# One PSUM tile of eight banks in place of four tiles of two banks, in a block-causal attention followed by a gated convolution layer

## The chip, the cores and the metric

The kernel runs on one core of one Trainium2 chip. The metric is device time in microseconds (us), lower is better: 213.19 us is the median of three runs of the kernel before (213.16 to 213.46).

## What is computed

```python
# attention: q, k, v are (8, 8, 576, 64) fp32
scores = scale * np.matmul(q, k.transpose(0, 1, 3, 2))      # scale = 1/8
mask = block_i >= block_j                                   # blocks of 64 positions
scores = np.where(mask, scores, -1000000000.0)
attn = np.exp(scores - np.max(scores, axis=-1, keepdims=True))
attn = attn / (np.sum(attn, axis=-1, keepdims=True) + 1e-09)
x = np.matmul(attn, v)                  # then reshaped to (8, 576, 512)
# gated layer: a causal convolution of 5 taps per channel makes the gate
gate_pre[:, s] = sum(conv_w[k] * xp[:, s + k] for k in range(5))   # xp: x with 4 rows of zeros ahead
gate = 1.0 / (1.0 + np.exp(-gate_pre))
out = (gate * (x @ w_val)) @ w_out      # w_val, w_out: (512, 512)
```

## The kernel before

The 64 heads are taken as 32 pairs, p = 0 to 31, four pairs to a batch. For two pairs at a time, 576 KB of q and of k are loaded (L171 to L182), cast to fp16 by GpSimd (`cq`, L212), and transposed by VectorE (`tq`, L246); the values come in 128 KB pieces (`Lv`, L191) and are cast by GpSimd (`cv`, L224). TensorE forms scores (`s`, L276) with 32-row tiles of the array, two heads to a pair of PSUM banks. ScalarE takes the exponential of both banks in one instruction (`e`, L288) and writes fp16 to `pt`; GpSimd clears the masked corner of it (`m`, L293 to L298). TensorE multiplies with the values (`av`, L304): 15 matmuls of 65 columns for one head, into one bank, where column 64 is the softmax sum. VectorE normalizes that bank (`n`, L317 a reciprocal `rc`, L318 a multiply into `x`). A pair's result is transposed, by TensorE and a VectorE copy (`xtr`, L325; `xt`, L338) or by a DMA (`xd`, L332), into `xt`.

The gated layer works on ten blocks of rows (`ORDER`, L343). For each, TensorE forms the convolution with diagonal matrices (`cn`, L354, four banks), ScalarE takes a tanh of two banks at a time (`th`, L382), TensorE multiplies with `w_val` (`val`, L386, one bank), VectorE multiplies gate and value (`gv`, L394, out of that bank), TensorE multiplies with `w_out` (`o`, L398, one bank), and ScalarE or VectorE copies the result out (`oc`, L406, which does it in the helper at L230) for the store (`st`, L413). Nearly all matmuls are recorded in the helper `mm`, so they carry L109.

The order of the work is written out by hand, in two strings at the head of the file, `START` and `PLAN`. Each word is one step: `av.13.1@4` is head 1 of pair 13 into bank 4, `val.2.0@5` the first quarter of `val` of block 2 into bank 5, `oc.0.2@A` a copy by ScalarE. The steps are recorded in that order on each engine (`tc.manual_schedule()`), and each engine runs its own in order; an instruction that waits holds up what is behind it on its engine. Which bank is used is thus fixed in the plan. The waits between engines are not written: the framework sets them, from what each instruction reads and writes of each tile.

PSUM has eight banks of 512 fp32 values per partition, 0 to 7. The kernel holds them as four tiles, B0 to B3, of two banks each; all accesses go through three small functions, `f32(i)` and `f16(i)` for one bank and `two(i, j, w)` for a pair of neighbours, which the exponentials and the tanh use:

```python
    def f32(i):
        return BK[i // 2][0:128, i % 2]
...
    def two(i, j, w):
        assert i % 2 == 0 and j == i + 1
        return BK[i // 2][0:128, 0:2, 0:w]
```

Of the kernel before, what the change touches and what calls it, by code (L numbers as in the profile page):

```python
# [87 lines left out]
def kernel(  # L88
# [11 lines left out]
    fp32 = mybir.dt.float32  # L100
# [4 lines left out]
    B, H, SEQ, D = q.shape  # L105
# [10 lines left out]
    psum = ctx.enter_context(tc.tile_pool(name="psum", bufs=1, space=bass.MemoryType.PSUM))  # L116
# [35 lines left out]
    tiny = const([128, 1], fp32, "tiny")  # L152


    BK = [psum.tile([128, 2, 512], fp32, tag=f"B{i}", name=f"B{i}") for i in range(4)]
    bank = {}

    def f32(i):
        return BK[i // 2][0:128, i % 2]

    def f16(i):
        return f32(i).bitcast(fp16)

    def two(i, j, w):
        assert i % 2 == 0 and j == i + 1
        return BK[i // 2][0:128, 0:2, 0:w]


    def load_qk(a, i, m):
# [93 lines left out]
    def steps(a, t, rows, m):  # L263
        qt, kt, z = qT[a % NQT], kT[a % NQT], kz[a % NQT].rearrange("p c g s -> p c (g s)")
        for r, b in zip(rows, m):
            bank["s", a, t, r] = b
        work = (((64, kt, 0, 64, 512), (0, z, 0, 0, 64), (0, z, 64, 512, 576)),
                ((0, kt, 128, 128, 576), (448, kt, 0, 512, 576)),
                ((0, kt, 256, 256, 576), (320, kt, 384, 384, 576)))[t]
        for w, (o, keys, g, x, y) in enumerate(work):  # L270
            for c in range(2):
                yield [(f32(b)[:, o:o + y - x], keys[32 * r:32 * r + 32, c, g:g + 128],
                        qt[32 * r:32 * r + 32, c, x:y], c == 0 and (t, w) != (0, 2), c == 1 and (t, w) != (0, 1))
                       for r, b in zip(rows, m)]
# [12 lines left out]
    def exps(a, t, r, m):  # L287
        nc.scalar.activation(out=pts[(2 * a + r) % NPT][0:128, 0:2, 512 * t:512 * t + 512],  # L288
                             in_=two(bank["s", a, t, 2 * r], bank["s", a, t, 2 * r + 1], 512),
                             func=AF.Exp, bias=0.0, scale=0.125)  # L290
# [13 lines left out]
    def av(p, h, m):  # L304
        b, g = divmod(p, 4)
        bank["av", p, h] = m[0]
        for i in range(5):
            for j in range(i + 1):
                o = last[j] if i == 4 else off[j] + 128 * i
                w = v16t[b % 2][0:128, 2 * g + h, 0:65] if j == 4 else v16s[p % NV][0:128, j, h, 0:65]  # L310
                mm(f32(m[0])[:, 65 * i:65 * i + 65], pts[p % NPT][0:128, h, o:o + 128], w,
                   start=(j == 0), stop=(j == i))
# [67 lines left out]
    def gate(n, r, m):  # L380
        w = width(n)
        nc.scalar.activation(out=ths[ORDER.index(n) % NTH][0:128, 2 * r:2 * r + 2, 0:w],  # L382
                             in_=two(bank["cn", n, 2 * r], bank["cn", n, 2 * r + 1], w),
                             func=AF.Tanh, bias=0.0, scale=0.5)
# [128 lines left out]
```

## Time and profile before

| what | value |
|---|---|
| median of three runs | 213.19 us |
| the profiled execution | 211.73 us |
| its span, first to last instruction | 209.9 us |
| VectorE (DVE) busy | 128.1 us, 61% |
| ScalarE (ACT) busy | 126.7 us, 60% |
| GpSimd (POOL) busy | 100.0 us, 48% |
| DMA queue q1: share of 16 engines' span, MB | 75.4%, 42.26 |
| mean granted clock of TensorE | 0.974 |

PE is TensorE's matmuls, PEld its weight loads, which overlap them; SP issues nearly all DMAs. Times in a timeline are microseconds from the start of the span. A group's "idle before, releaser" is how long the engine had stood still ahead of it, and what ended the longest of those waits. A busy matmul engine includes the drain of the pipeline after each run of matmuls.

### The profile page before, as it was taken

To read this page: it belongs to the slowest core of one execution; us is meant where nothing else is said; L and a number is where in the kernel's file an instruction comes from. 1 tells how busy PE (TensorE), PEld (TensorE's weight loads), DVE (VectorE), ACT (ScalarE), POOL (GpSimd) and SP (SyncE) were. 2 spreads that over 40 slices of the span, in tenths; PEclk is the share of its full clock that TensorE was granted. 3 is DMA by queue.
4 is the path that set the end of the run, shared out by engine and by line. 5 is a ranking of instruction groups with operands and counts; after the bars stand their busy time and mean duration, and the time that the engine had idled before them with its cause. 6 is when DMAs were issued, how large, how long until landed. Compare 5 with 4: busy or idle time off the path is not lost.

```text
span 209.9 us, 7311 instructions
## 1 busy us (share of the span) xinstructions
PE 166.1 (79%) x3082; PEld 101.0 (48%) x3082; DVE 128.1 (61%) x268; ACT 126.7 (60%) x147; POOL 100.0 (48%) x189
## 2 busy tenths in 40 slices
PE   3398679968789768988968878987787898979871
PEld 0235556635545444545555455543543575646430
DVE  2767475877756865766656757547447866562630
ACT  4398846957288736576866366764768685323331
POOL 5379776690391575383845253472345652200000
PEclk9999976999999979999999999999999999999999
DMA  5799899996029799990599579959997548952236
GB/s 143 181 372 277 230 326 359 369 247 226 2 66 245 142 219 323 313 282 10 116 228 323 98 122 297 328 144 107 312 320 204 108 86 228 206 150 101 105 131 169
DMA packets 61067, 43.12 MB, mean 205 GB/s; under 512 B 50917, under 2 KB 51173, under 8 KB 61034
## 3 DMA queue, kind: packets, MB, share of 16 engines
q1 hardware_dynamic: 60762, 42.26, 75.4%
q8 instruction: 24, 0.39, 0.7%
q10 hardware_dynamic: 272, 0.39, 0.6%
q14 instruction: 9, 0.07, 0.1%
HBM read 30.42 MB, written 9.44 MB: 190 GB/s over the span
## 4 chain that ended last, share of the span: by engine, by line
PE 50%; DVE 24%; DMA 11%; issue 4%; ACT 4%; SPq 2%; POOL 2%; DVEq 0%; POOLq 0%; ACTq 0%
PE B L109 49%; DVE x L318 7%; DVE gv L394 6%; DMA qks<-in_q_dram 6%; DVE kT L246 3%; DVE rc L317 3%; DMA vtst<-in_v_dram 2%; ACT osb L230 2%; DVE osb L230 2%; PE B L325 2%; SPq L179 1%; ACT th L382 1%; DMA qks<-in_k_dram 1%; DVE qT L246 1%; DMA vst<-in_v_dram 1%
## 5 line engine op out<-in xcount | busy, mean ns | idle before, releaser
L288 ACT ACTIVATE pt<-B 128x1024 f16<-128x1024 f32 x96 | 92.6, 1025 | 36.2 <-PE B L109 30.4
L230 POOL CAST qk<-qks 128x1152 f16<-128x1152 f32 (+1 forms) x33 | 44.3, 1350 | 23.9 <-DMA qks<-in_k_dram 10.0
L109 PE MATMUL B<-v,pt 128*128 128x65 f16 x896 | 37.7, 197 | 14.4 <-DVE x L318 6.2
L109 PEld LDWEIGHTS <-pt 128*128 128x128 f16 x960 | 36.0, 100 | 21.8 <-issue 14.8
L109 PE MATMUL B<-w_out,gv 128*128 128x512 f16 (+1 forms) x148 | 37.0, 380 | 6.5 <-DVE x L318 3.2
L109 PE MATMUL B<-xt,w_val 128*128 128x512 f16 (+1 forms) x160 | 36.0, 357 | 6.6 <-DVE gv L394 4.5
L109 PE MATMUL B<-qT,kT 32*128 32x448 f16 (+3 forms) x640 | 35.9, 304 | 6.2 <-DVE qT L246 4.1
L394 DVE SCALAR_TENSOR_TENSOR gv<-th,B 128x512 f16<-128x512 f32 (+1 forms) x40 | 24.8, 629 | 18.0 <-PE B L109 14.5
L318 DVE TENSOR_TENSOR x<-B,rc 128x320 f16<-128x320 f32 x64 | 31.5, 492 | 2.2
L317 DVE RECIPROCAL rc<-B 128x5 f32<-128x5 f32 x64 | 12.1, 190 | 29.2 <-PE B L109 26.5
L109 PEld LDWEIGHTS <-kT 32*128 32x128 f16 x640 | 17.2, 96 | 24.1 <-issue 10.4
L296 POOL MEMSET pt<- 64x384 f16 x32 | 13.2, 413 | 29.3 <-ACT pt L288 28.0
L382 ACT ACTIVATE th<-B 128x1024 f32<-128x1024 f32 (+1 forms) x20 | 17.7, 938 | 14.2 <-PE B L109 14.2
L230 ACT COPY osb<-B 128x512 f32<-128x512 f32 (+1 forms) x22 | 12.2, 569 | 22.4 <-PE B L109 18.4
L109 PEld LDWEIGHTS <-w_val 128*128 128x128 f16 x160 | 14.5, 97 | 20.1 <-issue 8.8
L109 PEld LDWEIGHTS <-gv 128*128 128x128 f16 x148 | 13.5, 98 | 19.0 <-issue 8.4
L246 DVE STREAM_TRANSPOSE kT<-qk 128x576 f32<-128x576 f32 (+2 forms) x18 | 20.4, 1131 | 3.4 <-POOL qk L230 3.3
L246 DVE STREAM_TRANSPOSE qT<-qk 128x576 f32<-128x576 f32 (+2 forms) x18 | 20.3, 1130 | 2.4 <-POOL qk L230 1.4
L224 POOL CAST v<-vst 128x512 f16<-128x512 f32 x32 | 19.5, 617 | 4.3 <-DMA vst<-in_v_dram 3.4
L230 DVE COPY osb<-B 128x512 f32<-128x512 f32 x15 | 10.2, 688 | 12.4 <-PE B L325 5.6
L295 POOL COPY pt<-pt 128x128 f16<-128x128 f16 x32 | 9.4, 295 | 11.7 <-ACT pt L288 11.4
L109 PE MATMUL B<-xt,DG 32*32 32x512 f16 (+1 forms) x800 | 13.8, 357 | 0.5 <-DVE x L318 0.3
(44 smaller groups left out, 99.8 us busy)
## 6 DMA issues: line engine op xcount, KB each, us to landing
qks<-in_q_dram SPq DMA_DIRECT2D x15, 576.0 KB, 6.3
qks<-in_k_dram SPq DMA_DIRECT2D x15, 576.0 KB, 5.2
vst<-in_v_dram SPq DMA_DIRECT2D x64, 128.0 KB, 4.6
out_dram<-osb SPq DMA_DIRECT2D x32, 256.0 KB, 3.4
vtst<-in_v_dram SPq DMA_DIRECT2D x8, 128.0 KB, 5.8
w_st<-in_moe_w_val_dram SPq DMA_DIRECT2D x2, 512.0 KB, 5.7
osb<-in_moe_w_out_dram SPq DMA_DIRECT2D x2, 512.0 KB, 7.7
out_dram<-osb SPq DMA_DIRECT2D x6, 128.0 KB, 3.1
```

The costliest lines, as they stand in the source:

```text
L109: nc.tensor.matmul(out=out, lhsT=lhsT, rhs=rhs, start=start, stop=stop, skip_group_check=True)
L224: nc.gpsimd.tensor_copy(out=v16s[p % NV][0:128, 0:4, 0:2, 0:64], in_=vst[p % NVS][0:128])
L230: (eng.copy if eng is nc.scalar else eng.tensor_copy)(out=o, in_=i)
L246: nc.vector.transpose(out=(qT, kT)[i][a % NQT][ps, :, t:t + 32 * w].bitcast(fp32).rearrange("p c (x n) -> p c n x", n=w // 2), in_=qk16[(2 ...
L288: nc.scalar.activation(out=pts[(2 * a + r) % NPT][0:128, 0:2, 512 * t:512 * t + 512], in_=two(bank["s", a, t, 2 * r], bank["s", a, t, 2 * ...
L295: nc.gpsimd.tensor_copy(out=pt[0:128, 0:2, 1536:1600], in_=pt[0:128, 0:2, 0:64])
L296: nc.gpsimd.memset(pt[64:128, 0:2, 0:1536].rearrange("p h (t s) -> p h t s", t=3)[:, :, :, 0:64], 0.0)
L317: nc.vector.reciprocal(out=rc[0:128], in_=O[:, :, 64:65])
L318: nc.vector.tensor_tensor(out=x16[p % NX16][0:128, 0:5, h, 0:64], in0=O[:, :, 0:64], in1=rc[0:128].to_broadcast([128, 5, 64]), op=ALU.mult)
L325: nc.tensor.transpose(out=f16(m[0])[:, 128 * i:128 * i + 128], in_=x16[p % NX16][0:128, i, 0:2, 0:64], identity=ident16[0:128, 0:128])
L382: nc.scalar.activation(out=ths[ORDER.index(n) % NTH][0:128, 2 * r:2 * r + 2, 0:w], in_=two(bank["cn", n, 2 * r], bank["cn", n, 2 * r + 1], w),
L394: nc.vector.scalar_tensor_tensor(out=gvs[z % NG][0:128, x, 0:w], in0=ths[z % NTH][0:128, x, 0:w], scalar=1.0, in1=f32(bank["val", n, x])[: ...
```

## The change

The four tiles become one tile `BB` of eight banks. The three functions pick the same banks by the same numbers out of it; no other line differs, and the plan, the steps and the bank numbers stay.

```diff
-    BK = [psum.tile([128, 2, 512], fp32, tag=f"B{i}", name=f"B{i}") for i in range(4)]
+    BB = psum.tile([128, 8, 512], fp32, tag="B", name="B")
     bank = {}
 
     def f32(i):
-        return BK[i // 2][0:128, i % 2]
+        return BB[0:128, i]
 
     def f16(i):
         return f32(i).bitcast(fp16)
 
     def two(i, j, w):
         assert i % 2 == 0 and j == i + 1
-        return BK[i // 2][0:128, 0:2, 0:w]
+        return BB[0:128, i:i + 2, 0:w]
```

## The prediction

> **What bounds the kernel now.** I read the busy time first, then three long stretches, then who waited for whom on PE and DVE, then a few microseconds of the timeline.
>
> ```profile
> PE 166.1 (79%) x3082; PEld 101.0 (48%) x3082; DVE 128.1 (61%) x268; ACT 126.7 (60%) x147; POOL 100.0 (48%) x189
> ```
>
> ```profile
> core 0: us, PE busy (x) PEld busy (x) DVE busy (x) ACT busy (x) POOL busy (x), PEclk, DMA share, GB/s
> 0.00:20.00 20.00, 12.04 (x139) 5.50 (x140) 12.68 (x30) 12.08 (x14) 12.68 (x27) 1.00 0.83 242
> 20.00:200.00 180.00, 149.92 (x2929) 93.60 (x2926) 114.23 (x236) 112.25 (x129) 87.28 (x163) 0.97 0.78 204
> 200.00:210.00 10.00, 4.11 (x22) 1.89 (x20) 1.23 (x3) 2.40 (x5) 0.00 (x0) 0.97 0.50 157
> ```
>
> PE is the busiest engine. The reader is to see that from 20 to 200 us it works 149.9 of 180 and stands still for 30.1; the ends (filling, last stores) are not what the change touches. So the question is what ends those 30.1 us.
>
> ```profile
> PE B L109 <- DVE x L318: 11.9, 16, 1.8
> PE B L109 <- DVE gv L394: 7.4, 10, 1.9
> PE B L109 <- DVE xt L338: 3.4, 4, 1.2
> PE B L325 <- DVE x L318: 2.4, 4, 0.9
> ```
>
> ```profile
> DVE rc L317 <- PE B L109: 26.5, 28, 2.4
> DVE gv L394 <- PE B L109: 14.5, 12, 3.6
> ```
>
> (engine, line, waited for: us in all, times, longest.) PE waits for DVE, and DVE, only 61% busy, waits for PE: 26.5 us ahead of reciprocals alone. Two engines that wait for each other are bound by the latency of the round trip, not by either one's work. The timeline shows what the round trip is made of.
>
> ```profile
> 89.01 0.59 PE L109 MATMUL B<-v,pt 128*128 128x65 f16 x14 [0.17 <-ACT osb L230]
> 89.44 0.19 PE L109 MATMUL B<-v16t,pt 128*128 128x65 f16 x1
> 89.47 1.03 PE L109 MATMUL B<-xt,w_val 128*128 128x512 f16 x4
> ...
> 91.90 0.59 PE L109 MATMUL B<-v,pt 128*128 128x65 f16 x14 [0.80 <-DVE gv L394]
> ```
>
> ```profile
> 90.53 0.20 DVE L317 RECIPROCAL rc<-B 128x5 f32<-128x5 f32 x1 [1.08 <-PE B L109]
> 90.76 0.49 DVE L318 TENSOR_TENSOR x<-B,rc 128x320 f16<-128x320 f32 x1
> 91.17 0.68 DVE L394 SCALAR_TENSOR_TENSOR gv<-th,B 128x512 f16<-128x512 f32 x1
> ```
>
> The plan reads `av.13.1@4 val.2.0@5 ... av.13.0@4`. The 15 `av` matmuls fill bank 4 by 89.63. Their reciprocal starts only at 90.53, after the four `val` matmuls, which write bank 5: they end at 90.50. Then the next `av` into bank 4 starts at 91.90, after the `gv` that reads bank 5, though `x`, the last reader of bank 4, ended at 91.25. Both waits are for the other bank of the same tile. **The two-bank tile is one thing to wait for.**
>
> **What the change does, part by part.** The programs as built can be listed with the count each instruction waits for. Order and operands are the same on all five engines; SP and POOL have the same waits, but for one store's semaphore. On DVE, 58 instructions wait for a smaller PE count; by the trace the matmul they then wait for ends 1.1 us earlier on average. In the example the reciprocal waits for count 1250 in place of 1254 (four `val` matmuls fewer), and the `av` for `x` in place of `gv`. No wait of the new program is for anything later than the old one's.
>
> *False waits on PE.* I laid the list beside PE's idle stretches over 0.25 us between 20 and 200. In 17 of them, 16.4 us together, the wait that ended last is no longer in the program; in 21, 11.5 us, it stays; the rest of the 30.1 is crumbs. What is late next in the 17 is the earlier DVE instruction, as in the example: `x` would start at 89.63 + 0.04 + 0.23 and end by 90.4, while PE works on other banks until 91.1, so its 0.80 goes whole. I take 15.5 of 16.4.
>
> *Kept waits on PE.* They are for results that PE needs (`x` before its transpose, `xt` before the convolution) or for the true reader of a bank. But their producers start earlier: 43 of DVE's idle stretches in this part, 49.6 us, ended with a wait that is gone, 1.15 us each, against 0.55 for a kept stall of PE. Where PE has other work between, the stall goes; where it needs x at once (reciprocal 0.20 and multiply 0.49 right behind its own matmuls), it stays. Ends: 0 and 11.5. I take 8, as DVE's lead is twice the stall.
>
> *Clock.*
>
> ```profile
> 20.00:30.00 10.00, 6.85 (x144) 5.82 (x141) 4.89 (x14) 7.74 (x9) 7.40 (x17) 0.92 0.95 264
> 30.00:40.00 10.00, 9.46 (x222) 6.58 (x221) 6.92 (x17) 6.38 (x8) 6.49 (x12) 0.74 1.07 371
> ...
> 70.00:80.00 10.00, 7.89 (x150) 4.87 (x149) 6.15 (x14) 4.19 (x5) 5.95 (x13) 0.83 0.95 201
> 80.00:90.00 10.00, 9.03 (x186) 5.28 (x186) 6.93 (x12) 7.44 (x9) 4.17 (x7) 1.00 1.08 328
> ```
>
> The third column from the end (PEclk) is the granted clock: 0.92, 0.74 and 0.83, so 10 x (0.08 + 0.26 + 0.17) = 5.1 us of PE time are lost, behind stretches with little PE work (6.85 of 10; PE still for 1.83 at 76.4). With fewer gaps some of it should not occur. Ends 0 and 5.1; I take 3, nearer the upper row. [...]
>
> *What is added.* Five semaphore waits (one on PE, four on DVE), and 35 more signals on PE and 25 on DVE. A wait row lasts 21 ns, 0.1 us in all; DVE instructions whose wait had ended long before start 0.08 us ahead of their predecessor's end, as those without a wait do. No row shows DVE on one bank of a tile while PE writes the other; `x` takes 0.49 beside PE at work on other tiles and without. From 0 to 60 x 21 ns = 1.3 us; I take 0.1.
>
> *DMA.* SP's order is unchanged, but the same 42 MB must pass in less time. In the seven 10 us stretches of 20 to 200 whose DMA share is 0.95 or more, PE's idle time is 11.6 us. If full queues held PE there, up to 11.6 of the gain would not come. The stalls in them are put down to DVE, not DMA, so I give back 1.5.
>
> **Sum**, against the profiled execution's 211.73: -15.5 - 8 - 3 + 0.1 + 1.5 = -24.9, that is 186.8. It lies 1.46 under the median of the runs; added, **188.3**, say 188. Ends: all idle time and all clock gone, 211.7 - 30.1 - 5.1 + 1.5 = 178; only the 16.4, less half of the DMA's 11.6, no clock, 213.2 - 10.6 = 203.
>
> **Rivals.**
> - *DMA takes over* (0.2). SP's loads become the wait behind POOL's casts: DMA packets already fill 0.78 of the middle, 140 of 180 us; at 156 us it would be 0.90. For it: seven stretches at 0.95 or more. Against: from 50 to 60 us the share is 0.07, because SP itself waits for a store. Gain 24.9 - 10.1 = 14.8: about 198.
> - *PE is filled* (0.2). All DVE latencies hide, PE's 150 us follow without gaps and at full clock: 178 to 183.
> - *Nothing happens* (0.02). It would if the false waits were covered by true ones. Against: 17 PE stalls of 0.25 to 1.93 us that end with them. 213.2.
> - *Slower through the clock* (0.05). The lowest clock, 0.74, lies in the densest stretch but one (9.46 of 10 busy). If dense work drew a low clock, PE's 150 us at 0.97 would be 150 x 0.97 / 0.74 = 197 us in the middle without any gap, 17 over the 180: 230 us. It decides from a clock of 150 x 0.97 / 180 = 0.81 down. Against: 80 to 90 has 9.03 busy at 1.00, and others like it.
>
> **How the numbers follow.** The forecast proper, 183 to 195, has 0.53; the chances beside the rivals are above. 178 to 203 takes in all but the clock, the nothing, and the edges of the others. Faster by over 0.2% (what a measurement of this kernel can tell): 0.93; within it 0.02; slower 0.05.
>
> **What would show it.** Right: DVE's wait for PE ahead of reciprocals falls from 26.5 to under 12 us, PE's waits for `x` and `gv` from 21.7 to under 8, PE busy at 88% or so with nearly the same 166 us, the clock at 0.98 or over. Wrong: PE idle under other names (POOL casts, kT, DMA) for 15 us or more, DMA shares at 1.0 in most slices, or a clock under 0.95.

## The result

The changed kernel takes **178.02 us** (median of four runs, 177.27 to 180.15); the kernel before, run beside it, 213.18 (210.57 to 213.46). The ratio is 0.836, 95% interval 0.827 to 0.846. The forecast was 188, the range 178 to 203: the sign was right, the time lies below the forecast proper of 183 to 195 and at the very bottom of the range, and 35 us came where 25 were forecast. The profiled execution of the changed kernel happens to be the slowest of its four, 180.15 us; the table of terms below uses it, and the text behind it says what that adds.

Busy time of the changed kernel, from its page:

```profile
PE 159.1 (89%) x3082; PEld 97.5 (55%) x3082; DVE 125.1 (70%) x268; ACT 126.0 (71%) x147; POOL 100.2 (56%) x189
```

The same three stretches as before: the middle now ends at 170 us.

```profile
0.00:20.00 20.00, 12.33 (x128) 5.33 (x128) 13.22 (x30) 11.51 (x14) 12.28 (x26) 1.00 0.80 238
20.00:170.00 150.00, 143.51 (x2936) 90.47 (x2937) 111.21 (x237) 112.29 (x130) 87.89 (x163) 0.99 0.95 245
170.00:180.00 10.00, 3.24 (x19) 1.67 (x17) 0.69 (x1) 2.22 (x5) 0.00 (x0) 0.83 0.51 156
```

PE stands still for 6.5 us of the middle, where it was 30.1. The number of instructions is the same (3082 matmuls, 268 on DVE), the DMA share has gone from 0.78 to 0.95, and the clock from 0.97 to 0.99. Who still waits for whom, first PE, then DVE:

```profile
PE B L109 <- DVE qT L246: 4.3, 3, 3.5
PE B L109 <- ACT pt L288: 2.0, 5, 0.6
PE B L109 <- issue: 1.6, 2, 1.4
PE B L109 <- DVE x L318: 1.6, 1, 1.6
...
PE B L109 <- DVE gv L394: 0.4, 1, 0.4
```

```profile
DVE rc L317 <- PE B L109: 11.8, 15, 2.1
DVE gv L394 <- PE B L109: 6.9, 6, 3.3
```

The 21.7 us in which PE waited for `x` and `gv` are 2.2 (0.2 of it ahead of L325, not shown). What leads the list now, `qT`, is the start of the kernel: 4.1 of its 4.3 us lie ahead of 20 us. The place of the prediction's example, in the changed kernel, PE and then DVE:

```profile
75.67 0.60 PE L109 MATMUL B<-v,pt 128*128 128x65 f16 x14
76.11 0.20 PE L109 MATMUL B<-v16t,pt 128*128 128x65 f16 x1
76.14 1.03 PE L109 MATMUL B<-xt,w_val 128*128 128x512 f16 x4
...
77.71 0.60 PE L109 MATMUL B<-v,pt 128*128 128x65 f16 x14
```

```profile
76.44 0.19 DVE L317 RECIPROCAL rc<-B 128x5 f32<-128x5 f32 x1
76.67 0.49 DVE L318 TENSOR_TENSOR x<-B,rc 128x320 f16<-128x320 f32 x1
77.21 0.69 DVE L394 SCALAR_TENSOR_TENSOR gv<-th,B 128x512 f16<-128x512 f32 x1
```

The reciprocal now starts at 76.44, in the middle of the four `val` matmuls (76.14 to 77.17), which write the other bank. And the next `av` starts at 77.71, with no idle time ahead of it, while `gv`, which reads the other bank, runs until 77.90.

### The profile page after: what moved, and what is told of

It is laid out like the page before. It is cut to its first block, busy times and chain, and to the rows that moved or that the text cites. A ratio compares the mean times of both kernels' runs of the same rounds, so it can differ in the third digit from the quotient of the medians.

```text
span 178.3 us, 7316 instructions
## 1 busy us (share of the span) xinstructions
PE 159.1 (89%) x3082; PEld 97.5 (55%) x3082; DVE 125.1 (70%) x268; ACT 126.0 (71%) x147; POOL 100.2 (56%) x189
## 3 DMA queue, kind: packets, MB, share of 16 engines
q1 hardware_dynamic: 60762, 42.26, 90.3%
## 4 chain that ended last, share of the span: by engine, by line
PE 45%; DMA 20%; DVE 9%; SPq 8%; ACT 7%; issue 5%; POOL 2%; ACTq 1%; POOLq 0%; DVEq 0%
PE B L109 43%; DMA qks<-in_q_dram 8%; DMA out_dram<-osb 6%; DMA qks<-in_k_dram 6%; ACT pt L288 5%; SPq L191 5%; POOL qk L230 2%; DVE x L318 2%; DVE qT L246 2%; PE B L325 2%; DVE gv L394 2%; DVE kT L246 2%; ACT osb L230 1%; DVE kz L230 1%; SPq L179 1%
## 5 line engine op out<-in xcount | busy, mean ns | idle before, releaser
L230 POOL CAST qk<-qks 128x1152 f16<-128x1152 f32 (+1 forms) x33 | 44.4, 1352 | 26.9 <-DMA qks<-in_k_dram 12.1
L109 PE MATMUL B<-qT,kT 32*128 32x448 f16 (+3 forms) x640 | 34.9, 296 | 7.7 <-DVE qT L246 4.3
L109 PEld LDWEIGHTS <-pt 128*128 128x128 f16 x960 | 33.3, 97 | 7.3 <-issue 2.7
L109 PE MATMUL B<-xt,w_val 128*128 128x512 f16 (+1 forms) x160 | 36.6, 363 | 0.3 <-issue 0.2
L109 PE MATMUL B<-v,pt 128*128 128x65 f16 x896 | 35.7, 194 | 0.7 <-ACT pt L288 0.4
L109 PE MATMUL B<-w_out,gv 128*128 128x512 f16 (+1 forms) x148 | 35.8, 373 | 0.1
L317 DVE RECIPROCAL rc<-B 128x5 f32<-128x5 f32 x64 | 11.8, 184 | 11.8 <-PE B L109 11.8
L109 PEld LDWEIGHTS <-DG 32*32 32x32 f16 x800 | 8.9, 88 | 8.0 <-issue 6.6
```

The costliest lines, as they stand in the source:

```text
L109: nc.tensor.matmul(out=out, lhsT=lhsT, rhs=rhs, start=start, stop=stop, skip_group_check=True)
L230: (eng.copy if eng is nc.scalar else eng.tensor_copy)(out=o, in_=i)
L317: nc.vector.reciprocal(out=rc[0:128], in_=O[:, :, 64:65])
```

## The experiments

Four kernels keep the one tile of eight banks and write the old waits back, kind by kind; two cut work out of the changed kernel to see what bounds it now, one does both, two do the same to the kernel before, one takes tiles of another size, and two try for more. The run of the kernel before that stands beside them gave 210.7 to 211.4 in the median.

### All three kinds of wait written back

```diff
+    def reads(ins, *banks):
+        for b in banks:
+            if True and b ^ 1 not in banks and b ^ 1 in wrote:
+                hold(ins, [wrote[b ^ 1]])
+            if True and b ^ 1 not in banks:
+                hold(ins, [o for o in unread.get(b ^ 1, []) if o.ins.engine != ins.ins.engine])
...
+    def writes(ins):
+        b = used[-1]
+        mine = unread.pop(b, [])
+        if True:
+            late = {str(o.ins.engine): o for o in unread.get(b ^ 1, []) if o not in mine and o not in held}
+            held.extend(late.values())
+            hold(ins, late.values())
```

`b ^ 1` is the neighbour bank of bank `b`. The first `if` is kind 1, a reader waits for TensorE's last write to the neighbour. The second is kind 3, a reader waits for the other engine's readers of the neighbour. The one in `writes`, which runs with each matmul, is kind 2: TensorE waits for readers of the neighbour. `hold` adds a dependency by hand (`tc.add_manual_dep`). With all three, DVE's, ACT's and PE's waits are those of the kernel before but for some ten, and PE's sit on the weight load ahead of the matmul.

> One tile of eight banks, as in the changed kernel, with the three kinds of wait for the other bank of a pair written back by hand: a reader waits for TensorE's last write to the neighbour bank, TensorE waits for the neighbour bank's last readers, and a reader waits for a reader of the neighbour bank on the other engine. Theory (the waits are the whole effect): the time of the kernel before comes back, 209 to 215 us, and the reciprocals' wait for PE is 26 us again. Rival (the single tile itself, its place in PSUM or how it is addressed, makes the kernel faster): it stays at 178, within 2 us.

Measured: 213.73 us, ratio to the kernel before 1.0075 (1.002 to 1.013). DVE's waits are back, and so are PE's:

```profile
DVE rc L343 <- PE B L134: 28.4, 28, 2.4
DVE gv L420 <- PE B L134: 15.4, 13, 3.6
```

```profile
PE B L134 <- DVE x L344: 12.0, 16, 1.8
PE B L134 <- DVE gv L420: 7.6, 11, 1.5
```

(L343 is the reciprocal here, L344 the multiply into `x`, L420 `gv`.) The tile and its addresses are those of the fast kernel, the waits those of the slow one, and the time is the slow one's, to 0.2 to 1.3%. So the waits are the whole effect; the rival falls.

### One kind at a time

```diff
-            if True and b ^ 1 not in banks:
+            if False and b ^ 1 not in banks:
...
-        if True:
+        if False:
```

Each of the next three kernels keeps one kind alone: two of the three conditions above are switched off. The lines are those that leave kind 1.

> Only the first kind is written back: VectorE and ScalarE, ahead of reading a bank, wait for TensorE's last write to the neighbour bank. Theory A (both directions make one round trip, so each alone costs about half of the 35 us, and the two together more than their sum): 188 to 198. Theory B (the readers' side carries it, since 26.5 us of the old waits stood ahead of reciprocals): 205 or more. Theory C (TensorE's side carries it): under 183.

> Only the second kind: TensorE, ahead of writing a bank, waits for the readers of the neighbour bank. Theory A (each direction about half): 183 to 194, somewhat less than the readers' side, since a false wait of TensorE is no longer than one or two VectorE instructions (0.7 to 1.3 us) where a reader's is up to thirty matmuls. Theory B (the readers' side carries it): under 182. Theory C (TensorE's side carries it): 205 or more.

> Only the third kind: ScalarE waits for VectorE's reading of the neighbour bank and VectorE for ScalarE's; 19 instructions get such a wait. Theory: 178 to 180, next to nothing, since ScalarE reads the neighbour bank in few copies only. Rival (ScalarE's copies and exponentials behind these waits are what TensorE's banks wait for): 184 or more.

| written back | median us | over 178.02 | ratio to before (95%) |
|---|---|---|---|
| kind 1, readers wait | 197.10 | 19.1 | 0.934 (0.927 to 0.942) |
| kind 2, TensorE waits | 185.46 | 7.4 | 0.881 (0.871 to 0.892) |
| kind 3, reader for reader | 179.98 | 2.0 | 0.853 (0.843 to 0.862) |
| all three | 213.73 | 35.7 | 1.008 (1.002 to 1.013) |

The first two times lie in the ranges of theory A: each direction costs its part, the readers' side more. "About half of the 35 us" fits kind 1 alone. 19.1 + 7.4 + 2.0 is 28.5, less than the 35.7 of all three, but the third column compares runs that were not made together: the kernel before took 213.18 beside the changed kernel and 211.44 beside these. By the ratios, less 0.836, the three are 0.098 + 0.045 + 0.017 = 0.160 and all together 0.172; with 0.836 known to 0.01, it is not shown that together they cost more than their sum. The third kind alone is next to nothing, as its theory has it: its interval overlaps the changed kernel's. PE's own waits show why kind 1 matters although PE never waits for a false reason there; the kernel with kind 1 alone:

```profile
PE B L134 <- DVE x L344: 4.6, 11, 0.8
PE B L134 <- DVE qT L272: 4.2, 2, 3.7
PE B L134 <- DVE gv L420: 3.4, 8, 0.9
PE B L134 <- DVE osb L256: 3.3, 6, 0.9
```

(L256 is the copy of results.) PE waits for `x`, `gv` and the copies by true need, because DVE was held up ahead of them.

### Two tiles of four banks

```diff
-    BB = psum.tile([128, 8, 512], fp32, tag="B", name="B")
+    BK = [psum.tile([128, 4, 512], fp32, tag=f"B{i}", name=f"B{i}") for i in range(2)]
...
-        return BB[0:128, i]
+        return BK[i // 4][0:128, i % 4]
...
-        return BB[0:128, i:i + 2, 0:w]
+        return BK[i // 4][0:128, i % 4:i % 4 + 2, 0:w]
```

> Two tiles of four banks; nothing else. Theory (a tile of less than all banks is one thing to wait for, so the wait grows with the tile): far slower than four tiles of two, 250 to 320 us, since a reader then waits for TensorE's work in three other banks. Rival (larger tiles are better, whatever their number, as the change goes from two banks to eight): between 178 and 213.

Measured: 353.02 us, one run. The direction is the theory's, the size is above its bounds. The page shows a part that the expectation left out:

```profile
PE 224.2 (64%) x3082; PEld 124.4 (35%) x3082; DVE 130.3 (37%) x268; ACT 129.8 (37%) x147; POOL 99.9 (28%) x189
...
PEclk9975555865559988896656598895655989979997
```

PE works for 64% of the span only, and its clock is 0.755 in the mean: the same 3082 matmuls take 224 us of busy time where the fast kernel's take 159. DVE's wait for PE ahead of reciprocals, 26.5 us before, is 64.2 here. Larger tiles are not better in themselves: with two banks 213, with four 353, with all eight 178. In this kernel a tile of two or of four banks is one thing to wait for, and the tile of all eight is tracked bank by bank. The waits and the times show that it is so; why it is so stays open.

### What bounds the changed kernel

```diff
-        for h in range(2):
+        for h in range(2 if p < NVS else 0):
```

This is "few values", in the loads of the values (`NVS` is 5); the next is "one tap", in the convolution:

```diff
-        for kk in range(5):
+        for kk in (4,):
...
-                       start=(kk == 0), stop=(kk == 4))
+                       start=True, stop=True)
```

> The changed kernel without 27 of the 32 loads of values (pairs 5 to 31 use the rows of an earlier pair that lie in the same buffer): 7 of 43 MB and 27,648 of 61,067 DMA packets less, about a quarter of the DMA engines' time; no other instruction is taken out. Theory P (TensorE is filled now, DMA is covered): 175 to 178. Theory D (DMA, with a share of 0.95 of the middle, is the bound now): 160 or less. Between them, both are near: 168 to 175.

> The changed kernel with one tap of the convolution in place of five: 640 matmuls of 32 rows less, by the row of 80 in 1.57 us about 11.5 us of TensorE's work; no load is taken out. Theory P (TensorE filled): 166 to 169, nearly all of it comes through. Theory D (DMA bound): 175 to 178.

> The changed kernel with both cuts: 27 of 32 loads of values left out (buffers reused) and one tap of the convolution in place of five. Alone they gave 176.2 and 175.4. Theory (TensorE and the DMA engines are both near full, and either takes over when the other is relieved): together well more than the sum of 2 and 3 us, 166 to 170. Rival (neither bounds it; what is left is latency through ScalarE, VectorE and GpSimd): 172 to 175.

Measured: few values 176.20 (ratio 0.835, 0.828 to 0.843, the changed kernel's own), one tap 175.41 (172.02 to 175.77), **both 166.59** (0.790, 0.787 to 0.794). Theory P was right of the values and wrong of the tap, though one of the four runs of one tap, at 172.02, lies between its theories. The chains that ended last tell more; changed kernel, few values, one tap, both:

```profile
PE 45%; DMA 20%; DVE 9%; SPq 8%; ACT 7%; issue 5%; POOL 2%; ACTq 1%; POOLq 0%; DVEq 0%
```

```profile
PE 73%; DVE 7%; ACT 6%; issue 4%; POOL 3%; DMA 3%; SPq 2%; POOLq 0%; ACTq 0%; DVEq 0%
```

```profile
PE 29%; DMA 27%; DVE 14%; POOL 10%; ACT 6%; SPq 6%; issue 5%; POOLq 1%; ACTq 0%; DVEq 0%
```

```profile
PE 59%; ACT 15%; SPq 7%; DMA 7%; DVE 5%; issue 3%; POOL 2%; ACTq 0%; POOLq 0%; DVEq 0%
```

With fewer loads the end hangs on PE for 73% of the span; with fewer matmuls PE's busy time falls by 9 us (159.1 to 150.1), and DMA has 27% of the chain in place of 20. Relieved alone, each gives 2 to 3 us in the median: few values nothing at all by the ratio, one tap 5 us if its one run at 172.02 is set against the changed kernel's fastest, 177.27. Together they give 11.4, or 0.046 of the ratio, 9.8 us. So TensorE and the DMA engines are both near full.

### The same cuts before the change

> The kernel before, with one tap in place of five, the same 11.5 us of TensorE's work less. Theory (a chain of round trips through TensorE and VectorE, TensorE's work on it about half of the span and the convolution with it): 202 to 206, most of it comes through here too, since these matmuls stand in TensorE's own line. Rival (TensorE only waits, its work is off the path): 211 or more.

> The kernel before without the same 27 loads of values (buffers reused). Theory (DMA is covered before the change, where its share of the middle is 0.78): 209 to 213, within 1% of the kernel before. Rival (DMA holds TensorE up there already, so that part of the gain is DMA's): 206 or less.

Measured: one tap 205.98 (ratio 0.977, 0.970 to 0.985), few values 210.39 (0.996, 0.993 to 1.000). The values behaved as expected: DMA was covered. About 5 us came through of the matmuls left out, within the bounds given. Of the estimated 11.5 us that is not "most of it", of the 6.9 by which PE's busy time fell (166.1 to 159.2) it is. That the rest lay beside other engines' work is argued, not shown.

### Two tries for more

In `PLAN`, each of the words `Lqk.6.*` to `Lqk.15.*` (loads of q and k) is moved up to 15 words ahead, in the second try up to 30, but not past the cast that frees its buffer. The second has six staging buffers too:

```diff
-    NQS, NVS, NQ16, NQT, NV, NPT, NX16, NG, NTH, NO = 5, 5, 3, 2, 4, 6, 4, 3, 2, 5
+    NQS, NVS, NQ16, NQT, NV, NPT, NX16, NG, NTH, NO = 6, 5, 3, 2, 4, 6, 4, 3, 2, 5
```

> The changed kernel with the q and k loads of pairs 6 to 15 moved up to 15 steps of the plan ahead, past stores, value loads and DMA transposes on SP's queue, never past the cast that frees their buffer. Theory (GpSimd's casts wait 24 us for these loads, and each is behind an SP instruction that waits for another engine): 173 to 176. Rival (the DMA engines are full, the order of what they move does not matter, or it delays the values): 177 to 180.

> As the run before, with up to 30 steps and six staging buffers for q and k in place of five. Theory: 171 to 175, more than with five buffers, whose casts bound the earliest issue. Rival: 177 to 180 as there.

Measured: 180.80 (ratio 0.857, 0.853 to 0.862) and 177.33 (0.840, 0.836 to 0.844), against the changed kernel's 0.836 (0.827 to 0.846): the first is slower, the second the same. GpSimd's waits for q and k fell from 12.1 + 11.8 us (k and q) to 3.9 + 8.4 and 2.0 + 4.7, and nothing came of it. The traces show one reason that the rival names, later values: GpSimd's waits for the values rose from 5.7 us to 15.4 and 16.5. What the first lost is not settled, since the second delays the values as much and loses nothing. Neither version beats the changed kernel.

## Why the prediction was right, and where it was short

Term by term, from the two profiled executions, 211.73 and 180.15 us, 31.6 apart:

| term | forecast | measured |
|---|---|---|
| PE's idle time, middle (15.5 + 8) | -23.5 | 30.1 to 6.5: -23.6 |
| PE's idle time, both ends | 0 | 13.8 to 12.7: -1.1 |
| PE's busy time (clock) | -3 | 166.1 to 159.1: -7.0 |
| added waits | +0.1 | not to be seen |
| given back to DMA | +1.5 | not to be seen |
| sum | -24.9 | -31.6 |

- **False and kept waits**: right in mechanism, as the kernel with all waits written back shows, and their sum right in size; the signs came too (26.5 to 11.8 us ahead of reciprocals, 21.7 to 2.2 for `x` and `gv`). That most of the kept stalls go too because their producers start earlier is what the kernel with kind 1 alone shows from the other side: with DVE held up, PE waits again. The split into 15.5 and 8 was not measured. It is not one by kind of wait: TensorE's false waits alone cost 7.4 us, the readers' alone 19.1, and the 15.5 took for granted that DVE starts earlier as well.
- **Clock**: under-sized, and only part of a larger term. That 3 of the 5.1 us would come back was the author's estimate; no row of the kernel before shows it. 1 - clock times span is 5.5 us before (0.974 of 209.9) and 2.5 after (0.986 of 178.3), so 3.0 is the clock in this pair, as taken. The prediction's own count, by stretches of 10 us in the middle, gives 5.1 before and 1.7 after (30 to 40 us, at 0.83, is the only one under 1.00 from 20 to 170 us), so 3.4. The prediction has no term for the other 4 us of busy time. In the traces a matmul of 512 columns lasts 0.38 us and four in a row 1.03, so each overlaps the one behind it by 0.16 us ((4 x 0.38 - 1.03) / 3); the last before a gap overlaps none and counts in full. Counted in the two traces, PE's work falls into 65 unbroken stretches before and 22 after, so fewer such ends are in it. That this is all of the 4 us is not shown. So "nearly the same 166 us" failed: this is the step that made the forecast short.
- **DMA** gives nothing back that can be told: without a fifth of the DMA work (q1 was busy 90.3% of 178.3 us, with few values 72.0% of 175.5) the changed kernel is at 0.835 in place of 0.836. But with a share of 0.95 there is little room left, as one tap and both cuts show. One of the prediction's signs of being wrong did appear, DMA shares at 1.0 in most slices: 8 of the 15 stretches of 10 us from 20 to 170 us have 1.03 to 1.13. It held PE up little: PE stands still for 6.5 us there.
- **The offset** from the profiled execution to the median was taken as +1.46, from the kernel before; here the median lies 2.1 under the profiled execution. These 3.6 us are the rest of the way from 188 to 178: 1.5 + 4.0 + 1.1 + 3.6 make 10.2. Much of the 2.1 is the clock again: the profiled execution lost 2.5 us by it, the other three, at 0.996, 0.996 and 1.000, 0.7 and less. So in those runs the clock gave about 5 against the 5.5 of the kernel before, near the upper end of its term. Which execution is profiled is chance, and so is that part of the miss.
- **The range** caught the result by luck. Its lower end, 178, starts from the profiled execution's 211.7 and leaves out the 1.46 that the forecast adds; with it the end would be 179.5, above the 178.02 measured. That end also has no term for a shorter busy time beyond the clock.
- **The rivals.** "PE is filled", 178 to 183 with 0.2, is close to what happened: 6.5 us without work are left in the middle, at a clock of 0.99. "Nothing happens" and "DMA takes over" did not. "Slower through the clock" has the sign wrong: the mean clock was 0.755 with PE busy 64% of the span, 0.964 to 0.983 in kernels with 77 to 79%, 0.981 at 84%, 0.986 to 0.996 from 86% up. Its stretch at 0.74 is the densest of all by busy time (9.46 of 10), not the densest but one; and at a low clock busy time is longer for the same work (a `w_out` matmul has 491 ns in the mean in the kernel with four-bank tiles, at 0.755, and 373 in the changed kernel, at 0.986). In the changed kernel eight of the 15 stretches of 10 us from 20 to 170 us have PE busy for 10.00, each at a clock of 1.00.

## What to carry to other kernels

Where two engines that are not full wait for each other, lay the list of waits beside the trace and ask of each stall whether the wait that ended it is for data that the instruction needs: here 17 stalls of PE and 43 of DVE were for the neighbour bank. What a framework tracks may be a tile and not a bank, so how PSUM is cut into tiles sets waits that no line of the kernel says; look at the built program after each such choice. And once the latency is gone, relieve the two fullest engines together: alone, 9 us of matmuls or a fifth of the DMA work gave 2 to 3 us in the median, together 11.

## What was not expected of the hardware

That the kernel with the most idle time of PE also ran it at the lowest clock. In the kernel with tiles of four banks the same matmuls were busy for 224 us in place of 159, at a clock of 0.755 in place of 0.986. So beside the 127 us in which PE stood still (351.2 less 224.2), another 65 were lost while it worked; as an estimate the clock has 49 of them (159 x 0.986 / 0.755 is 208).

When is seen in the clock row of that kernel's page, above: 5 or 6 tenths in 17 of its 40 slices, 7 to 9 in the others. What brings the clock down there is not shown.
